# Two transformer layers on one core: the MLP's second products by seven block products, behind all its first products

## The chip, the cores and the metric

The kernel runs on one core of a Trainium2 chip. The metric is device time in microseconds, the median of three runs; before the change it is 3550.99 us (3549.95 to 3551.67). The core has a matmul engine (PE, with its weight loads PEld), three engines for elementwise work (DVE, ACT, POOL), a queue that issues transfers (SP), an on-chip memory (SBUF) and eight accumulation banks (PSUM) into which PE writes.

## What is computed

`x` has 2048 rows of 640. Attention (32 heads of 20) and an MLP follow each other twice, with the same weights in both layers:

```
x = x + attention(layernorm(x), wqkv, wo)
x = x + mlp(layernorm(x), w1, b1, w2, b2)
x = x + attention(layernorm(x), wqkv, wo)
x = x + mlp(layernorm(x), w1, b1, w2, b2)

mlp(y): h = relu(y @ w1 + b1) ** 2        # 2048 x 1536
        out = h @ w2 + b2                 # 2048 x 640
```

All arrays are float32. This document is about the MLP: "first products" are `y @ w1`, "second products" are `h @ w2`.

## The kernel before

**Numbers in two parts.** PE multiplies in a shortened float format. Each operand is therefore split into a high part and the remainder (`split_to`, line 254: ACT casts, DVE subtracts), and every product is made of three matmuls, high x high, high x low and low x high (`THREE`, line 323).

**Memory.** One pool holds 42 slots of 128 partitions x 1024 words ("slot", line 67), a second one 11 tiles of 640 words ("xtile", line 78). The weights lie in pieces, several to a slot, in the class `Split` (line 118). They are split once, on POOL, by `prep_job` (line 838) during the attention of layer one (steps t = 0 to 15 of 32, three times in each), saved to DRAM by `save_full`, and loaded again into slots when a stage needs them. The second weights `w_2` (line 202) are 48 pieces of 320 columns, in 16 slots. The pieces of the first weights `w_1` are 128 columns wide, 120 of them in 15 slots.

**Order.** The program's order is the order on each engine: nothing is rescheduled, and each engine and SP's queue work strictly in turn. Work that is to lie beside matmuls is put between them by hand: a list `steps` of small functions, of which `side()` (line 1364) takes one after each chain of matmuls.

**The MLP.** The rows are taken in four blocks of 512 (`qb`). `mlp` (line 1286) handles one block, in two halves of F (`fh`), six tiles of 128 each. For a tile of F it makes a chain of 15 matmuls of 512 columns into a bank (`chain`, line 333; 5 row groups of `w1` x 3). ACT adds the bias and applies ReLU (line 1301), DVE squares (line 1302), and `split_to` makes the two parts of `h`. After six tiles the second products follow: for each half of the 640 columns (`hf`) and each of four row tiles (`i`) a chain of 18 matmuls of 320 columns, with 128 rows of `h` as the loaded weights and a piece of `w_2` streaming. DVE adds the bank to the row tile `x` (line 1332), to which POOL has added `b2` (line 1308). After the last half SP stores `x`. So first and second products alternate every six tiles, and `h` stays in SBUF.

While a block runs, the next block's rows are loaded, normalised and turned (`turned_rows`, line 302: statistics, scaling and a 32 x 32 transposition on DVE, a trip through DRAM) and split (`parts`, line 292). In the last block of layer one the side work is instead `second()` (line 1403), the front of layer two: normalisation and transposition on PE of its first row blocks (`front`, line 448), with the banks from the ring `ps_all`.

**Counts.** Per block 12 x 15 = 180 first matmuls and 2 x 2 x 4 x 18 = 288 second ones; four blocks and two layers make 1440 and 2304. All of them have line 336 in the profile, told apart by their operands (`xnT,w` and `w,h`).

Of the kernel before, what the change touches and what calls it, by code (L numbers as in the profile page):

```python
# [8 lines left out]
F32 = mybir.dt.float32  # L9
# [7 lines left out]
P = 128  # L17
S = 2048
D = 640
# [2 lines left out]
DH = 20  # L22
KD = D // P
NF = F // P
QB = 512
NQB = S // QB
NG = H // 4
# [6 lines left out]
NBLK = NG * NQB  # L34
NSLOT = 42
NX = 11


@with_exitstack
def tile_layers(  # L40
# [26 lines left out]
    def slot(shape, dtype, label):  # L67
        return arena.tile(shape, dtype, tag="slot", name=name(label))
# [9 lines left out]
    def xtile(label):  # L78
        return xpool.tile([P, D], F32, tag="x", name=name(label))
# [124 lines left out]
    def at_2(f, hw, hf):  # L204

        return (((f // 6) * 2 + hf) * 6 + f % 6) * 2 + hw
# [12 lines left out]

    def put_rows(sp, raw, k, eng_hi, eng_lo):  # L220
        if sp is w_2:
            for hf in range(2):
                part = raw[:, hf * HALF : (hf + 1) * HALF]
                sp.put(part, at_2(k, 0, hf), at_2(k, 1, hf), 1, eng_hi, eng_lo)
        else:
            sp.put(raw, k * 4, k * 4 + 2, 2, eng_hi, eng_lo)

    d_qk = dram.tile([2, 2, D, S], F32R, name="d_qk")
    d_kd = dram.tile([2, 2, 2 * P, QB], F32R, name="d_kd")
# [4 lines left out]
    d_s = dram.tile([NBLK, 4, QB], F32, name="d_s")  # L234
    d_r = dram.tile([NBLK, 4, QB], F32, name="d_r")
    d_t = dram.tile([4, P, D], F32, name="d_t")
    d_x = [dram.tile([S, D], F32, name=f"d_x{i}") for i in range(3)]

    def stats(x):
# [14 lines left out]
    def split_to(dst_hi, dst_lo, src):  # L254

        nc.scalar.copy(dst_hi, src)
        nc.vector.tensor_sub(dst_lo, src, dst_hi.bitcast(F32))
# [62 lines left out]
    def new_rows():  # L320
        return [slot([P, 2, QB], F32R, "xnT") for _ in range(KD)]
# [456 lines left out]
    def finish(t, acc):  # L778
# [52 lines left out]

    jobs = (
        [("o", k) for k in range(KD)]
        + [("1", j) for j in range(NF)]
        + [("2", f) for f in range(NF)]
    )

    def prep_job():

        if raws:  # L840
            kind, i, raw = raws.pop()
            if kind == "1":
                w_1.put(raw, i * 10, i * 10 + KD, KD, pool_hi, pool_lo)
            else:
                put_rows(w_o if kind == "o" else w_2, raw, i, pool_hi, pool_lo)
        if jobs:
            kind, i = jobs.pop(0)
            raws.append((kind, i, raw_cols(w1, i) if kind == "1" else raw_rows(wo if kind == "o" else w2, i)))

# [250 lines left out]
    def attention(first, x_src, first_rows):  # L1100
# [27 lines left out]
        def begin(i):  # L1128

            t, u = divmod(i, NKT)  # L1130
            g, qb = divmod(t, NQB)
            if u == 3:
                q_t.pop(t - 1, None)
            if u == 1:
                if t + 2 < NBLK and t + 2 not in q_t:
                    load_q(t + 2)
            if u % 4 == 1 and qb == 0:
                k_t.pop((g - 1, u // 4), None)
                for h in (0, 1, 2, 3) if g else (1, 2):
# [8 lines left out]
            if first and t < 16 and u == 8:  # L1148
# [134 lines left out]
            xnt.append(t)  # L1283
        return xnt

    def mlp(qb, xnt, x_mid, x_dst, side, nxt):

        xs, res = [], None
        for fh in range(2):
            hs = []  # L1290
            for f in range(fh * 6, fh * 6 + 6):
                dst = ps_all("pu")
                chain(dst, [
                    (w_1.piece(f * 10 + hw * KD + k), xnt[k][:, hx, :])
                    for k in range(KD)
                    for hw, hx in THREE
                ])
                if qb == NQB - 1:
                    w_1.past(f * 10 + 9)
                r = xtile("r")[:, :QB]  # L1300
                nc.scalar.activation(r, dst, AF.Relu, bias=b1_t[:, f : f + 1])  # L1301
                nc.vector.tensor_mul(r, r, r)
                h = slot([P, 2, QB], F32R, "h")
                split_to(h[:, 0, :], h[:, 1, :], r)
                hs.append(h)
                if fh == 0 and f in (1, 2, 3, 4):
                    x = row_tile(x_mid, qb * 4 + f - 1)
                    nc.gpsimd.tensor_add(x, x, b2_t)
                    xs.append(x)
                side()  # L1310
            for hf in range(2):
                c = slice(hf * HALF, (hf + 1) * HALF)
                dsts = [ps_all("y") for _ in range(2)]

                def down(i, part=None):
                    chain(dsts[i][:, :HALF], [
                        (hs[f % 6][:, hx, i * P : (i + 1) * P], w_2.piece(at_2(f, hw, hf)))
                        for f in range(fh * 6, fh * 6 + 6)
                        for hx, hw in THREE
                    ], part)  # L1320

                for i in range(4):
                    if i > 1:
                        dsts.append(ps_all("y"))
                    if hf or i > 1:
                        down(i)
                    elif i == 0:
                        for part in (slice(15), slice(15, 18)):
                            for j in range(2):
                                down(j, part)  # L1330
                    x, dst = xs[i], dsts[i]
                    nc.vector.tensor_add(x[:, c], dst[:, :HALF], x[:, c])
                    if fh == 1 and hf == 1:
                        r0 = (qb * 4 + i) * P
                        dma(nc.sync, x_dst[r0 : r0 + P, :], x)
                    side()
                    if (fh, hf, i) == (1, 0, 0) and nxt:
                        res = new_rows()
                        for j in range(4):
                            parts(res, j, nxt.pop(0))  # L1340
            if fh == 0 and qb == NQB - 1:
                w_2.past(at_2(5, 1, 1))
        return res

    def layer(first, x_a, x_m, x_e, front_0, ahead):
        xs = []
# [34 lines left out]
                all_steps()  # L1381
        w_o.drop()
        xnt = transposed(rows)
        for s in range(w_2.n):
            w_2.load(s)
        for qb in range(NQB):
            rows = []
            if qb + 1 < NQB:
                norm = turned_rows(qb + 1, x_m, rows)
                step = lambda norm=norm: next(norm, None)  # L1390
                both = lambda step=step: (step(), step())
                steps.extend([None] * 6 + [step, both, both, step, step, step, step, both])
            elif ahead:
                some = lambda: [next(ahead, None) for _ in range(2)]
                steps.extend([None] * 7 + [some] * 19 + [lambda: next(ahead, None)])
            xnt = mlp(qb, xnt, x_m, x_e, side, rows if qb + 1 < NQB else None)
            if qb + 1 < NQB:
                all_steps()
        steps.clear()
        w_1.drop()  # L1400
        w_2.drop()

    def second():


        yield from front(0, d_x[1], ps_all)
        for n, _ in enumerate(front(1, d_x[1], ps_all)):
            if n < 5:
                w_qk.load(n)
            yield  # L1410
        yield from front(2, d_x[1], ps_all)
        yield from front(3, d_x[1], ps_q)

    def begin_first():
# [54 lines left out]
```

## Time and profile before

| what | us |
|---|---|
| median of three runs | 3550.99 |
| span of the profiled execution | 3549.7 |
| layer one: projections and attention | to 1373 |
| layer one: output projection | 1373 to 1445 |
| layer one: MLP | 1447 to 1786 |
| layer two: projections and attention | 1786 to 3139 |
| layer two: output projection | 3139 to 3211 |
| layer two: MLP | 3211 to 3546 |

The times of the stages are read from the chain of waits. The profile lists an execution's span; its groups give for each line the engine, the operation, output<-input with shapes, the count, then busy time in us and the mean of one in ns, and the idle time before them with what ended it. A matmul's recorded duration overlaps the next one's, so the spacing of matmuls is read from a run of them, not from the mean.

### The profile page before, as it was taken

How to read it: one execution, taken by the hardware profiler on the slowest of the kernel's cores; microseconds unless marked ns; L12 is line 12 of the kernel's file. 1: busy time of each engine (PE TensorE's matmuls, PEld its weight loads, DVE VectorE, ACT ScalarE, POOL GpSimd, SP SyncE). 2: the span in 40 equal slices, each digit the busy share in tenths (PEclk: the TensorE clock that was granted, in tenths of full speed). 3: DMA queues.
4: the chain of work that ended last, by engine and by line, in shares of the span. 5: the costliest groups of instructions: out<-in, count | busy, mean ns of one | idle time of the engine just before them, and what ended most of it. 6: DMA issues, size and time to landing. Idle time of an engine off the chain costs nothing.

```text
span 3549.7 us, 70872 instructions
## 1 busy us (share of the span) xinstructions
PE 3537.8 (100%) x25544; PEld 2147.2 (60%) x25544; DVE 2631.9 (74%) x5090; ACT 2694.4 (76%) x4712; POOL 820.3 (23%) x935
## 2 busy tenths in 40 slices
PE   9999999999999999999999999999999999999999
PEld 8998333333333336999989973333333333379998
DVE  8999888888888881445579988888888888715443
ACT  5888999999999994122248899999999999932221
POOL 4430344321211210122153201212121211202110
PEclk9999999999999999999999999999999999999999
DMA  7766455423112136622366652222222121366221
GB/s 258 231 209 184 147 167 161 129 76 79 55 48 62 53 103 217 240 75 75 104 205 227 197 165 71 75 79 58 70 82 57 43 60 52 107 233 220 75 82 38
DMA packets 281598, 431.87 MB, mean 122 GB/s; under 512 B 70948, under 2 KB 130084, under 8 KB 281248
## 3 DMA queue, kind: packets, MB, share of 16 engines
q1 hardware_dynamic: 280720, 425.64, 38.6%
q8 instruction: 203, 3.33, 0.4%
q10 hardware_dynamic: 528, 1.70, 0.2%
q14 instruction: 147, 1.20, 0.1%
HBM read 282.52 MB, written 144.68 MB: 120 GB/s over the span
## 4 chain that ended last, share of the span: by engine, by line
PE 96%; DMA 1%; ACT 1%; POOL 1%; issue 0%; SPq 0%; DVE 0%; ACTq 0%; POOLq 0%
PE banks L770 28%; PE banks L336 23%; PE banks L755 18%; PE banks L661 17%; PE banks L368 5%; PE banks L356 5%; PE banks L351 1%; ACT e L765 1%; PE banks L468 0%; SPq L76 0%; DMA d_qk<-ev 0%; DMA x<-in_A_x_dram 0%; DMA q<-d_qk 0%; DMA kd<-d_kd 0%; POOL xnT L271 0%
## 5 line engine op out<-in xcount | busy, mean ns | idle before, releaser
L765 ACT ACTIVATE e<-banks 128x512 f32<-128x512 f32 (+1 forms) x3416 | 2035.0, 691 | 55.6 <-PE banks L755 20.5
L672 DVE TENSOR_REDUCE mx<-banks 128x1 f32<-128x512 f32 x2560 | 1619.7, 684 | 321.0 <-PE banks L661 269.6
L770 PE MATMUL banks<-e,vg 128*32 128x512 f32 x8192 | 1093.4, 605 | 2.3 <-ACT e L765 2.1
L661 PE MATMUL banks<-k,q 60*128 60x512 f32 x3360 | 1059.6, 410 | 0.0
L755 PE MATMUL banks<-q,k 62*128 62x512 f32 x4096 | 1048.9, 441 | 1.3 <-ACT v L432 0.6
L755 PEld LDWEIGHTS banks<-q,k 62*128 62x128 f32 x4096 | 514.7, 184 | 748.3 <-ACT e L765 441.1
L661 PEld LDWEIGHTS banks<-k,q 60*128 60x128 f32 x3360 | 567.9, 185 | 195.4 <-ACT e L765 63.9
L701 DVE CUSTOM_DVE_ANT_0 rl<-banks,rl 128x512 f32<-128x512 f32 x736 | 476.9, 688 | 31.1 <-PE banks L661 6.8
L694 ACT ACTIVATE rl<-banks 128x512 f32<-128x512 f32 x736 | 399.6, 602 | 57.0 <-PE banks L661 45.3
L770 PEld LDWEIGHTS banks<-e,vg 128*32 128x32 f32 x8192 | 162.1, 108 | 353.0 <-issue 271.6
L1301 ACT ACTIVATE r<-banks,b_t 128x512 f32<-128x512 f32 x96 | 66.2, 689 | 364.4 <-PE banks L336 245.8
L336 PE MATMUL banks<-w,h 128*128 128x320 f32 x2304 | 341.2, 309 | 0.0
L336 PEld LDWEIGHTS banks<-w,h 128*128 128x128 f32 x2304 | 339.1, 188 | 1.2
L336 PE MATMUL banks<-xnT,w 128*128 128x512 f32 x1440 | 329.7, 389 | 0.0
L368 PE MATMUL banks<-xnT,wqk 64*128 64x512 f32 x1080 | 326.5, 392 | 0.0
L356 PE MATMUL banks<-xnT,wqk 64*128 64x512 f32 x1080 | 325.6, 393 | 0.0
L336 PEld LDWEIGHTS banks<-xnT,w 128*128 128x128 f32 x1440 | 269.5, 188 | 55.3
L814 POOL TENSOR_TENSOR few<-few,minus_t 128x16 f32<-128x16 f32 x62 | 179.8, 2900 | 234.3 <-DMA few<-d_s 228.5
L661 PE MATMUL banks<-kd,q 60*128 60x512 f32 x736 | 210.8, 398 | 0.8 <-ACT rl L694 0.5
L356 PEld LDWEIGHTS banks<-xnT,wqk 64*128 64x128 f32 x1080 | 199.2, 186 | 13.0 <-issue 1.7
L368 PEld LDWEIGHTS banks<-xnT,wqk 64*128 64x128 f32 x1080 | 201.2, 187 | 7.1
L268 POOL CAST mr<-nt 128x32 fp32r<-128x32 f32 x64 | 13.4, 210 | 813.6 <-DVE nt L727 813.6
(94 smaller groups left out, 2710.2 us busy)
## 6 DMA issues: line engine op xcount, KB each, us to landing
q<-d_qk SPq DMA_DIRECT2D x876, 80.0 KB
d_qk<-ev SPq DMA_DIRECT2D x80, 512.0 KB
k<-d_qk SPq DMA_DIRECT2D x444, 80.0 KB
x<-d_x SPq DMA_DIRECT2D x96, 320.0 KB
d_o<-ot SPq DMA_DIRECT2D x248, 80.0 KB
ot<-d_o SPq DMA_DIRECT2D x38, 512.0 KB
d_v<-v SPq DMA_DIRECT2D x32, 512.0 KB
vg<-d_v SPq DMA_DIRECT2D x32, 512.0 KB
```

What stands on the lines that cost most here:

```text
L336: nc.tensor.matmul(dst, a, b, start=(n == 0), stop=(n == last))
L356: top = nc.tensor.matmul(dst, a[:64], b[:64], start=start, stop=last)
L368: low = nc.tensor.matmul(dst, a, b, start=False, stop=last, skip_group_check=True)
L661: nc.tensor.matmul(dst, q_t[t][b : b + 60, p, sub * P : (sub + 1) * P], k_t[t // NQB, c][b : b + 60, p, :], start=True, stop=True,)
L672: nc.vector.tensor_reduce(maxima(t)[:, 2 * p + par, sub, c : c + 1], dst, axis=AX.X, op=ALU.max)
L694: nc.scalar.activation(r, dst, AF.Relu)
L701: nc.vector.tensor_tensor_reduce(out=r[par], in0=dst, in1=r[par], scale=1.0, scalar=LEAST, op0=ALU.add, op1=ALU.max, accum_out=maxima(t)[: ...
L755: nc.tensor.matmul(dst, k_t[t // NQB, kt // 4][b : b + 62, p, (kt % 4) * P : (kt % 4 + 1) * P], q_t[t][b : b + 62, p, :], start=True, stop ...
L765: nc.scalar.activation(dst, src, AF.Exp, scale=SCALE)
L770: nc.tensor.matmul(acc[32 * h : 32 * h + 32, :], v_t[t // NQB, kt // 8][:, kt % 8, 32 * h : 32 * h + 32], es[p][:, par, :], start=(kt == 0 ...
L814: nc.gpsimd.tensor_tensor(few, few, minus_t, op=ALU.pow)
L1301: nc.scalar.activation(r, dst, AF.Relu, bias=b1_t[:, f : f + 1])
```

## The change

The MLP is rewritten in three respects.

**All first products of a layer come ahead of its second products.** `up` makes the first products of a block. The squared tiles `r` are not split but stored to DRAM (`d_h`), two F tiles to a slot: tile j and tile j + 6, each with 4 row tiles, ordered so that a slot holds for two "units" of 256 rows the four blocks (row tile 0 or 1) x (F half 0 or 1). One sum and one difference that the scheme needs (`s`, and `r[:, :, 2]` in place) are made by DVE there; `s` goes to `d_h1`. A tile's store stands in SP's queue behind the next tile's activation. The stores come after the last addition that writes the tile.

**The second products go by seven block products (Strassen's scheme, in Winograd's form).** The class `Down` takes units of 256 rows: two row tiles, two halves of F, two halves of the columns. Instead of eight block products (144 matmuls) it makes seven (126 matmuls): `W11, T2, T1, T4` into four banks, then, after these have been read out to `u` and to the row tiles, `W21, W22, T3` accumulated onto three of the same banks. Six steps make a unit: two groups x three pairs of F tiles. `make` builds the operands of a step (sums of blocks on DVE, split by ACT and DVE) two steps ahead, `fetch` reads the tiles of the next unit back. Units alternate between banks 0 to 3 and 4 to 7. The addition of `b2` moves from POOL to DVE. In layer one the last 512 rows (two units) are done plainly, 144 matmuls each, in banks 0 to 3, while the front of layer two runs beside them in banks 4 to 7 (`ps_up`); their pieces `W12` are loaded in the place of `T1` to `T4`. In layer two all eight units go by seven products.

**The second weights are kept as eight block sets** instead of four: `W11, W12, W21, W22` and the sums `T1` to `T4`, 96 pieces in 32 slots. `put_pair` makes them from two raw tiles on POOL, in five portions per pair; the preparation therefore runs to step t = 21 (`LAST_PREP`) instead of 15. Pieces of the first weights are put in the order in which `up` uses them (`at_1`).

The diff, cut to its core:

```diff
+NP = NF // 2
+LAST_PREP = 22
...
+    ps_up = Ring(4, 5, 6, 7)
...
-    w_2 = Split("w2", HALF, NF * 4)
+    w_2 = Split("w2", HALF, NP * 16)
...
+    W11, T2, T1, T4, W21, W22, T3, W12 = range(8)
+    SECTIONS = ((W11,), (T2, T1, T4), (W21, W22), (T3,), (W12,))
...
+    def put_pair(f, a, b):
+        t = xtile("t")
+        one, two = slice(0, HALF), slice(HALF, D)
+        def put(p, part):
+            w_2.put(part, at_2(p, f, 0), at_2(p, f, 1), 1, pool_hi, pool_lo)
+        pool_lo(t[:, one], a[:, two], a[:, one])
+        pool_lo(t[:, two], b[:, two], t[:, one])
+        put(W11, a[:, one])
+        yield
+        put(T1, t[:, one])
+        put(T2, t[:, two])
+        yield
...
-            if first and t < 16 and u % 6 == 3:
+            if first and t < LAST_PREP and u % 6 == 3:
                 prep_job()
...
+    def up(qb, xnt, whole, side):
+        held = []
+        def store():
+            while held:
+                r, s = held.pop(0)
+                j = held.pop(0)
+                dma(nc.sync, d_h[qb, j]..., r...)
+                if whole:
+                    dma(nc.sync, d_h1[qb, j]..., s)
+        for j in range(NP):
+            r = slot([P, 2, 4, P], F32, "r")
+            for i in range(2):
+                f = j + i * NP
+                dst = ps_all("pu")
+                chain(dst, [...])
...
+                nc.scalar.activation(r[:, :, i::2, :], ..., AF.Relu, bias=b1_t[:, f : f + 1])
+                if i:
+                    s = None
+                    nc.vector.tensor_mul(r, r, r)
+                    if whole:
+                        s = xtile("s")[:, : 2 * P]
+                        nc.vector.tensor_add(s..., r[:, :, 2, :], r[:, :, 3, :])
+                        nc.vector.tensor_sub(r[:, :, 2, :], r[:, :, 0, :], r[:, :, 2, :])
+                    held.extend([(r, s), j])
+                else:
+                    store()
                 side()
+        return store
...
+        def make(self):
...
+            if grp == 0:
+                s = self.s[un, j]
+                nc.vector.tensor_sub(s[:, 1], s[:, 0], raw[:, :, 0, :])
+                b = self.parts(raw[:, :, 0::3, :], "hb")
+                a = self.parts(s, "ha")
...
+            elif grp == 1:
+                s = self.s.pop((un, j))
+                nc.vector.tensor_sub(s[:, 1], raw[:, :, 1, :], s[:, 1])
+                c = self.parts(raw[:, :, 1:3, :], "hc")
+                d = self.parts(s[:, 1], "hd")
...
+        def run(self, side):
+            for n, (un, grp, j) in enumerate(self.steps):
+                if j == 0 and grp != 1:
+                    b0 = 4 * (un % 2) if grp == 0 else 0
+                    dsts = [banks[:, b0 + b, :HALF] for b in range(4)]
+                    x1, x2 = self.x.pop(un)
+                    for x in (x1, x2):
+                        nc.vector.tensor_add(x, x, b2_t)
...
+                if n + self.LEAD < len(self.steps):
+                    self.make()
+                if grp == 2 or (grp, j) in ((0, 1), (0, 2), (1, 0)):
+                    self.fetch()
...
+                for p, b in order:
+                    for i in range(2):
+                        for hx, hw in THREE:
+                            self.mm(dsts[b], ops[p][:, hx, i],
+                                w_2.piece(at_2(p, lo_f + i, hw)), ...)
+                    if j == last_j:
+                        self.take(un, grp, b, dsts[b], u, x1, x2, c1, c2)
...
+        def take(self, un, grp, b, dst, u, x1, x2, c1, c2):
+            add = nc.vector.tensor_add
+            if grp == 0:
+                if b == 0:
+                    nc.scalar.copy(u[:, 0], dst)
+                elif b == 1:
+                    add(u[:, 1], dst, u[:, 0])
+                elif b == 2:
+                    add(x2[:, c2], dst, x2[:, c2])
+                else:
+                    add(x2[:, c1], dst, x2[:, c1])
+                    add(x1[:, c2], x1[:, c2], u[:, 1])
+            elif b == 0:
+                add(x1[:, c1], dst, x1[:, c1])
+                self.halves(un, x1)
+            elif b == 1:
+                add(u[:, 2], dst, u[:, 0])
+                for c in (c1, c2):
+                    add(x2[:, c], x2[:, c], u[:, 2])
+                self.store(un, 1, x2)
+            else:
+                add(x1[:, c2], dst, x1[:, c2])
+                self.halves(un, x1)
...
+        blocks = NQB if ahead is None else NQB - 1
+        down = Down(blocks, x_m, x_e)
+        coming = [s for s in range(w_2.n) if s not in slots_of(W12)]
...
+                wants = [4, 4, 3, 0, 0, 0, 3, 0, 0, 0, 0, 0] if qb == 0 else [0] * 12
+            else:
+                steps.extend([None] * 5 + [down.fetch, None, down.fetch, lambda: down.rows(0), down.make, down.fetch, down.make])
+                wants = [0, 2, 0, 2, 0, 2, 1, 2, 1, 2, 1, 2]
...
+        down.run(side)
```

More of the change, by code (lines that the diff above doesn't have):

```diff
@@ L220, in put_rows @@
     def put_rows(sp, raw, k, eng_hi, eng_lo):
[L221 to L226, printed above, removed]
+        sp.put(raw, k * 4, k * 4 + 2, 2, eng_hi, eng_lo)
+    def put_pair(f, a, b):
[10 more added lines that the diff above has]
+        yield
+        put(W12, a[:, two])
+        put(W21, b[:, one])
+        yield
+        put(W22, b[:, two])
+        pool_lo(a[:, two], b[:, two], a[:, two])
+        yield
+        put(T3, a[:, two])
+        pool_lo(t[:, two], b[:, one], t[:, two])
+        put(T4, t[:, two])
+        yield
     d_qk = dram.tile([2, 2, D, S], F32R, name="d_qk")
@@ L1298, in mlp @@
                 if qb == NQB - 1:
[L1299 to L1309, printed above, removed]
@@ L1310, in mlp @@
-                side()
[L1311 to L1335, printed above, removed]
-                    side()
[L1337 to L1340, printed above, removed]
@@ new lines, in layer @@
+            all_steps()
+        bring(99)
+        w_1.drop()
+        if ahead:
+            some = lambda: [next(ahead, None) for _ in range(2)]
+            per = 7 * NP // 2
+            one = lambda: next(ahead, None)
+            steps.extend([None] * (per * (2 * blocks - 1)))
+            last = [None] * per
+            for i in (0, 5, 7, 9, 11, 14, 16, 18, 20):
+                last[i] = one
+            last[13] = last[19] = one
+            steps.extend(last + [None] + [one] * 6 + [some] * 11)
@@ L1410, in second @@
             yield
-        yield from front(2, d_x[1], ps_all)
+        yield from front(2, d_x[1], ps_up)
         yield from front(3, d_x[1], ps_q)
```

214 lines of the change are left out of this document (183 added, 31 removed).

## The prediction, made before the changed kernel had run

> **What bounds the kernel now.** I read the page first, then the windows of the two MLP stages, then the chain of waits, then the groups by form. The page:
>
> ```profile
> span 3549.7 us, 70872 instructions
> ...
> PE 3537.8 (100%) x25544; PEld 2147.2 (60%) x25544; DVE 2631.9 (74%) x5090; ACT 2694.4 (76%) x4712; POOL 820.3 (23%) x935
> ...
> PE   9999999999999999999999999999999999999999
> ...
> DVE  8999888888888881445579988888888888715443
> ACT  5888999999999994122248899999999999932221
> ...
> PEclk9999999999999999999999999999999999999999
> ```
>
> PE is busy for 3537.8 of 3549.7 us and its granted clock is full from end to end. DVE and ACT have a quarter free, but that is an average. So I look at the two stages that the change rewrites (columns: stretch, length, busy time and count of PE, PEld, DVE, ACT, POOL, then clock, DMA share, GB/s):
>
> ```profile
> 1447.00:1735.00 288.00, 288.00 (x1622) 263.28 (x1621) 143.54 (x242) 67.50 (x146) 57.77 (x84) 1.00 0.34 115
> ...
> 3211.00:3546.00 335.00, 334.40 (x1889) 305.87 (x1889) 151.88 (x253) 77.36 (x161) 55.27 (x76) 1.00 0.28 97
> ```
>
> Here PE is busy throughout (288.00 of 288, 334.40 of 335) while DVE is at half and ACT at a quarter. The chain of waits (start, length, what) says the same:
>
> ```profile
> 1446.87 288.17 PE banks L336 x1620
> ...
> 1736.35 2.64 PE banks L336 x18
> ...
> 3213.52 332.34 PE banks L336 x1872
> ```
>
> Almost the whole of both MLP stages is one unbroken run of line 336 matmuls, so a matmul taken away is time taken away, so long as no other engine becomes late.
>
> The pace comes from the same rows. A chain of 18 second-product matmuls of 320 columns takes 2.64 us: **146.7 ns each**. The run of 332.34 us in layer two holds 1872 matmuls; 1152 second products at 146.7 ns are 169.0 us, which leaves 163.3 us for 720 first products of 512 columns: 226.8 ns each. The groups give the counts, for both layers together:
>
> ```profile
> L336 PE MATMUL banks<-w,h 128*128 128x320 f32 x2304 | 341.2, 309 | 0.0
> L336 PEld LDWEIGHTS banks<-w,h 128*128 128x128 f32 x2304 | 339.1, 188 | 1.2
> L336 PE MATMUL banks<-xnT,w 128*128 128x512 f32 x1440 | 329.7, 389 | 0.0
> ```
>
> Their means (309 and 389 ns) are longer than the spacing because matmuls overlap; I cost by the spacing.
>
> **What goes.** A unit is 256 rows of output. Plain, it takes 4 output blocks x 12 tiles of F x 3 matmuls = 144 matmuls, 21.12 us. By seven products it takes 7 x 6 x 3 = 126, or 18.48 us. Layer one does 6 units so and 2 plain, layer two does 8 so: 14 x 18 = **252 matmuls fewer, 252 x 0.1467 = 37.0 us**. First products, transposes and attention keep their PE instructions. This is the one gain; everything else below is a question of whether it stays hidden.
>
> The Trainium skill, "TensorE: Matmul & The Clock Gate", section "Back-to-back issue gap", gives an isolated spacing of N/2.4 + 2.5 ns, 135.8 ns at 320 columns, by which an estimate of the saving is 34.2 us; the same section has about 131 ns as a sustained spacing at 512 columns. The trace agrees with neither (146.7 ns at 320 columns, 226.8 at 512), and its spacing stands in the sum.
>
> **What is added: vector and scalar work.** The durations:
>
> ```profile
> L1302 DVE TENSOR_TENSOR r<-r 128x512 f32<-128x512 f32 x96 | 79.5, 828 | 131.2 <-ACT r L1301 129.8 <-DMA y<-d_t 1.3
> L257 DVE TENSOR_TENSOR h<-r,h 128x512 fp32r<-128x512 f32 x96 | 73.7, 767 | 66.0 <-ACT h L256 66.0
> L1301 ACT ACTIVATE r<-banks,b_t 128x512 f32<-128x512 f32 x96 | 66.2, 689 | 364.4 <-PE banks L336 245.8 <-issue 113.6 <-DMA y<-d_t 2.7
> L1332 DVE TENSOR_TENSOR x<-banks,x 128x320 f32<-128x320 f32 x128 | 61.3, 485 | 147.7 <-PE banks L336 132.9 <-POOL x L1308 13.6 <-issue 0.3
> ...
> L256 ACT CAST h<-r 128x512 fp32r<-128x512 f32 x96 | 59.6, 621 | 91.5 <-DVE r L1302 91.5
> L1308 POOL TENSOR_TENSOR x<-x,b_t 128x640 f32<-128x640 f32 x32 | 58.8, 1866 | 165.6 <-DMA x<-d_x 165.6
> ...
> L166 DVE TENSOR_TENSOR wqk<-raw,wqk 128x512 fp32r<-128x512 f32 x1 | 0.7, 685 | 0.0
> ...
> L166 DVE TENSOR_TENSOR wqk<-raw,wqk 128x256 fp32r<-128x256 f32 x1 | 0.4, 418 | 0.0
> ```
>
> ```profile
> L257 DVE TENSOR_TENSOR h<-r,h x96: 691/693/1296, 1452.5 to 3526.9; 128x512 fp32r<-128x512 f32 x96
> ```
>
> With nothing beside it the 128x512 subtraction takes 691 to 693 ns; 256 columns take 418, so one column is 1.04 ns. From that 1024 columns are estimated at 1.22 us and the 640-column bias addition at 0.82 us. Bounds: 0.685 us (512 columns) below, and 1.87 us above, the POOL row that did the same addition; I take 0.82, as it is DVE's own slope.
>
> In a unit by seven products, for each of three pairs of F tiles, the first four products need one 256 subtraction and two 512 ones (1.80 us of DVE), the last three need two of 256 and one of 512 (1.53 us): 3 x 3.33 = 10.0 us. Six additions from PSUM at 0.485 are 2.9 us, three of 320 columns in SBUF at about the same are 1.5 us, and two bias additions, which move here from POOL, are 1.6 us. **DVE: 16.0 us in a unit of 18.48 us**, 87%. ACT copies 3 x (512 + 512 + 512 + 256 columns) at 621 ns per 512, and one bank: some 7 us.
>
> 16.0 fits in 18.48, but DVE works in order, so I follow one unit from PE's start (0). The previous unit's last additions end at 1.5, the bias additions at 3.2, then operands two steps ahead: (first group, pair 2) ready at 5.0, needed at 7.04; (second group, pair 0) 6.5, needed 10.56; pair 1 8.0, needed 13.20. At 8.8 DVE stands behind PE for the evacuations until 11.5; then pair 2 13.1, needed 15.84; the next unit's pair 0 14.9, needed 18.48; pair 1 16.7, needed 22.0. The smallest margin is 2.0 us, so I cost it at nothing. Cover gone (each operation 15% longer), DVE sets the pace. The lead of two steps hides the casts too; the four banks of a unit alternate with the other four, so an evacuation has a whole unit before its bank comes again. Within a unit the second group adds onto three of these banks: bank 0 was copied 2.6 us earlier, bank 2's addition starts two products before and takes 0.49.
>
> In the first products ACT loses the cast (0.62 per tile). DVE loses the subtraction and gains, per pair of tiles, 256 columns twice: 6 x (1.22 + 0.84) = 12.4 us in a block of 180 x 0.2268 = 40.8 us. The next block's rows are normalised there as well:
>
> ```profile
> L244 DVE BATCH_NORM_STATS2 bst<-x 128x6 f32<-128x320 f32 x128 | 54.8, 470 | 21.9 <-DMA x<-d_x 19.2 <-DMA x<-in_A_x_dram 2.7
> ...
> L252 DVE TENSOR_SCALAR x<-x,mv 128x640 f32<-128x640 f32 x40 | 25.3, 659 | 1.3 <-POOL mv L248 1.2
> ...
> L277 DVE TENSOR_SCALAR y<-x,mv 128x640 f32<-128x640 f32 x24 | 22.3, 927 | 0.0
> ...
> L282 DVE STREAM_TRANSPOSE x<-y 128x640 f32<-128x640 f32 x24 | 20.3, 845 | 0.8
> L300 DVE TENSOR_TENSOR xnT<-y,xnT 128x128 fp32r<-128x128 f32 x48 | 20.1, 486 | 0.0
> ...
> L245 DVE BATCH_NORM_AGGREGATE mv<-bst 128x2 f32<-128x12 f32 x64 | 13.4, 209 | 2.2
> ```
>
> Four rows of that: statistics 4 x 1.15, turning 4 x 1.77, splitting 8 x 0.49, 15.6 us. Together 28 of 40.8, and PE has a ring of eight banks. The last row's split is issued a whole chain (3.4 us) before it is needed and takes some 1.5 us of ACT. Cost nothing; if late, 1 to 2 us at three block edges per layer.
>
> **What is added: transfers.** Per layer 24 stores of 512 KB, each read back later as much, and the 128 KB sums with them; 16 more weight slots are saved and 12 to 16 more loaded per layer. In the first-product block that is 3.75 MB per 40.8 us, some 100 GB/s; in a unit 1.9 MB of reads and 1.25 MB of rows, some 180 GB/s. The heaviest stretch now:
>
> ```profile
> 1447.00:1487.00 40.00, 40.00 (x226) 36.48 (x225) 20.24 (x39) 8.60 (x14) 8.99 (x12) 1.00 0.82 318
> ```
>
> 318 GB/s ran beside a PE that did not wait. The last block of layer two, with half of the second weights, tiles and stores, comes to about 13 MB in 40.8 us, near that figure; its last loads are needed only 10 us later. SP's order: a tile's store is queued behind the next tile's activation, and the reads of the next unit wait on the subtractions that free a slot. Behind such a read stand the next row reads and the output stores, which nobody needs within a unit; behind ACT's copy of a bank, which waits for PE, stand casts that are wanted two steps later. The tightest read is issued at 6.5 us of the unit and wanted at 13.1: it is free if it lands in 6.6 us. The nearest row that shows a slow landing is in the chain of waits, a wait for a store:
>
> ```profile
> 1843.80 9.19 DMA d_qk<-ev
> ```
>
> At that, a read would be 2.6 us late per unit, 2.6 x 14 = 36 us. The bytes alone, 640 KB at 318 GB/s, are 2.1 us. The ends are 2.1 and 9.19; I take the margin as enough, since a unit asks for little over half of 318 GB/s, and keep the 36 us for a rival.
>
> Slots: 42. In the first products 15 weight slots + 10 + 14 loaded + 3 for tiles is 42 exactly; in a unit 28 + 3 + 6 to 8 + 1, 38 to 40. Nothing spare, but each slot used again was released at least a step before.
>
> **Attention of layer one** gains POOL work to t = 22: six pairs x (8 splits + 4 subtractions) instead of 24 splits.
>
> ```profile
> L271 POOL TENSOR_TENSOR w<-raw,w 128x320 fp32r<-128x320 f32 x24 | 20.9, 870 | 1.9
> ...
> L268 POOL CAST w<-raw 128x320 fp32r<-128x320 f32 x24 | 10.8, 452 | 19.5 <-DMA raw<-in_B_w_dram 17.2 <-DMA q<-d_qk 2.3
> ```
>
> 84 us instead of 32, so 52 us more. During the present preparation, and after it:
>
> ```profile
> 500.00:600.00 100.00, 100.00 (x717) 38.64 (x717) 83.90 (x140) 97.23 (x166) 42.09 (x53) 1.00 0.50 153
> ...
> 900.00:1000.00 100.00, 100.00 (x718) 38.41 (x716) 83.82 (x138) 97.54 (x166) 19.53 (x18) 1.00 0.21 56
> ```
>
> 717 and 718 PE instructions per 100 us, with POOL at 42 and at 20 us: preparation costs nothing here, and I cost the rest of it at nothing (0 to 1 us).
>
> **Small costs.** At the hand-over from first to second products, the last tile's chain is 0.69 (ACT) + 1.22 + 0.84 + 1.80 = 4.6 us, against 3.52 us of PE work: 0 to 1.0 us per layer, as the first matmuls need only a part; 0.5 each, 1.0 in all. In layer one's last Strassen unit DVE also has the statistics and scaling of four rows (4.6 + 2.6), 22 us in 18.5; the lead of 5.3 us takes most: 0 to 3.5, I take 0.7. The four slots of the second weights that change there must land in 9.7 us: 4 x 480 KB are 6.2 us at 318 GB/s, nothing (3 us, once, if they queue). At the end, now
>
> ```profile
> 3545.89 0.49 DVE L1332 TENSOR_TENSOR x<-banks,x 128x320 f32<-128x320 f32 x1 [2.15 <-PE banks L336]
> ```
>
> the last addition follows the last matmul by one instruction; afterwards three additions stand before it and it ends about 0.2 us later. Sum: 1.9 us.
>
> The profiled execution shows no time but its span. 3549.7 - 37.0 + 1.9 = 3514.6; the median of the runs, 3550.99, is 1.3 above the span, which I add, so **3516 us**, 1.0% faster.
>
> **Rivals.**
> 1. *Late reads or slots*: PE waits a little in every unit. For it: slots full, SP in order. Against: 318 GB/s beside an unhindered PE. At 1 us a unit 3530; at 2.6 us 3552.
> 2. *Conversion sets the pace, and the kernel is slower.* The place is DVE's operand making in the 14 units. It begins when an operation takes 1.15 times its row; the gain is gone when a unit takes 21.12 us, at 16.0 x 1.32. For it, the same operations beside POOL:
>
> ```profile
> L1302 DVE TENSOR_TENSOR r<-r x96: 636/693/2098, 1451.1 to 3525.6; 128x512 f32<-128x512 f32 x96
> ```
>
> and the 1296 ns maximum of line 257. At 1296/693 a unit takes 29.9 us, 14 x 11.4 = 160 more: 3676. Against it: POOL has almost nothing to do in these units, its bias additions being gone. The Trainium skill, "SBUF — State Buffer", section "Who interferes with whom", says that a DVE instruction with two SBUF inputs and a GpSimd instruction that reads SBUF exclude each other for a whole instruction; the trace agrees (2098 against 693 ns), but by that rule an idle POOL costs nothing.
> 3. *The pace of the matmuls rises*, because a bank gets 6 matmuls in a row and not 18, and the load shows. At the load's own 188 ns, 2052 x 41 ns = 84 more: 3600. Against: the bank changes every 18 now and shows no gap.
> 4. *It does not do what it says*: the matmuls go, but waits at block edges and between units give the 37 us back: 3551.
>
> **Chances.** Forecast (3511 to 3524) 0.67; late reads 0.15, at 3530, up to 3545; conversion 0.10, at 3676, of which 0.02 near break-even; pace 0.04; nothing gained 0.04. About 0.2% (7 us) is what a measurement here can tell from no change. Faster 0.82, same 0.06, slower 0.12. The range 3511 to 3545 leaves out 0.18.
>
> **What would show it.** PE unbroken through both stages, 2052 second products at 146.7 ns: right. In the second products, PE waiting for a DVE subtraction (rival 2), with DVE over 95%; for a DMA into a tile, with DVE idle behind it (rival 1); PE busy with spacing over 150 ns (rival 3); attention longer than now, that preparation or slots cost after all. I would be wrong most easily by having summed queues that work in order as if their margins held in every unit.

## The result, and the profile after

The changed kernel takes 3516.18 us (median; 3515.69 to 3517.9) beside 3551.33 us for the kernel before: a ratio of 0.9902, 95% interval 0.9888 to 0.9916. The profiled execution has a span of 3516.1 us. The page of the changed kernel, in its lines for span, busy time and slices:

```profile
span 3516.1 us, 71077 instructions
...
PE 3504.1 (100%) x25292; PEld 2112.9 (60%) x25292; DVE 2732.5 (78%) x5326; ACT 2733.7 (78%) x4804; POOL 828.0 (24%) x975
...
PE   9999999999999999999999999999999999999999
...
DVE  8999888888888882566869988888888888825667
...
PEclk9999999999999999999999999999999999999999
```

PE is still busy almost without a break; DVE has gone from 74 to 78% and ACT from 76 to 78%, and the slices of the MLP, in which DVE had mostly 4 to 5 tenths, now have mostly 5 to 8. The windows of the changed kernel (first and second products of layer one, then of layer two; columns as before):

```profile
1446.00:1610.00 164.00, 164.00 (x729) 135.88 (x727) 90.72 (x151) 47.16 (x114) 32.74 (x60) 1.00 0.76 266
1610.00:1770.00 160.00, 160.00 (x1107) 159.88 (x1106) 123.58 (x248) 55.89 (x103) 16.69 (x29) 1.00 0.59 206
3201.00:3364.00 163.00, 163.00 (x721) 134.99 (x720) 94.21 (x160) 45.99 (x111) 32.36 (x60) 1.00 0.76 266
3364.00:3513.00 149.00, 148.26 (x1009) 147.64 (x1007) 115.55 (x232) 52.55 (x103) 0.00 (x0) 1.00 0.51 173
```

First and second products are now separate stretches, and PE is busy in all of them. The price of keeping `h` in DRAM, and of the added weight slots, is seen in the last column: 266 and 206 GB/s in layer one, 266 and 173 in layer two, where the stretches of the MLP before had 115 and 97. The chain of waits (start, length, what) has line 376 for first and line 1455 for second products:

```profile
1446.62 163.25 PE banks L376 x720
1609.87 114.40 PE banks L1455 x780
...
1769.54 3.44 PE banks L391 x15
...
3125.57 2.39 PE banks L376 x15
...
3200.85 163.23 PE banks L376 x720
3364.08 146.44 PE banks L1455 x996
```

720 first products take 163.25 us, 226.7 ns each, where 226.8 was worked out for the kernel before. The MLP of layer one lasts from 1446.62 to 1769.54, 322.92 us against 338.90. That of layer two begins at 3200.85, and its last matmuls stand in the timeline of PE at the end:

```profile
3511.22 1.04 PE L1455 MATMUL banks<-w,hc 128*128 128x320 f32 x6
```

They end at 3512.26, so the stage lasts 311.41 us against 332.34. Together **36.9 us less**; 252 matmuls at 146.7 ns are 37.0. The groups by form show the count:

```profile
L1455 PE MATMUL banks<-w,hb 128*128 128x320 f32 x504 | 83.2, 309 | 0.0
L1455 PE MATMUL banks<-w,hc 128*128 128x320 f32 x504 | 83.0, 309 | 0.0
L1455 PE MATMUL banks<-w,ha 128*128 128x320 f32 x504 | 80.8, 309 | 0.0
...
L1455 PE MATMUL banks<-w,hd 128*128 128x320 f32 x252 | 43.8, 309 | 0.0
...
L1455 PE MATMUL banks<-w,hh 128*128 128x320 f32 x192 | 42.7, 311 | 0.0
...
L1455 PE MATMUL banks<-w,hl 128*128 128x320 f32 x96 | 29.7, 309 | 0.0
```

504 + 504 + 504 + 252 + 192 + 96 = 2052, where there were 2304.

The span is 33.6 us shorter, not 36.9. The missing 3 us are outside the rewritten stages: layer two's projections and attention took 1353.01 us before (1785.77 to 3138.78) and 1356.03 now (1769.54 to 3125.57). At their start PE stood. The timeline and the window there:

```profile
1788.37 0.79 PE L701 MATMUL banks<-k,q 60*128 60x512 f32 x1 [0.86 <-DMA q<-d_qk]
```

```profile
1786.00:1796.00 10.00, 9.14 (x57) 6.94 (x56) 6.45 (x11) 1.13 (x2) 0.00 (x0) 0.83 0.64 213
```

PE stood 0.86 us for a tile of queries, and the granted clock of those 10 us is 0.83, which is 1.7 us at full clock. Whether the change causes this is one of the questions below.

### The profile page after: what moved, and what is told of

It is laid out like the page before. It is cut to its first block, busy times and chain, and to the rows that moved or that the text cites. A ratio compares the mean times of both kernels' runs of the same rounds, so it can differ in the third digit from the quotient of the medians.

```text
span 3516.1 us, 71077 instructions
## 1 busy us (share of the span) xinstructions
PE 3504.1 (100%) x25292; PEld 2112.9 (60%) x25292; DVE 2732.5 (78%) x5326; ACT 2733.7 (78%) x4804; POOL 828.0 (24%) x975
## 4 chain that ended last, share of the span: by engine, by line
PE 96%; DMA 2%; ACT 1%; POOL 0%; DVE 0%; issue 0%; SPq 0%; POOLq 0%; ACTq 0%; DVEq 0%
PE banks L810 28%; PE banks L795 18%; PE banks L701 18%; PE banks L376 13%; PE banks L1455 9%; PE banks L396 6%; PE banks L408 5%; PE banks L391 0%; PE banks L508 0%; ACT e L805 0%; DMA x<-d_x 0%; DMA x<-in_A_x_dram 0%; SPq L78 0%; DMA few<-d_s 0%; DMA o<-d_r 0%
## 5 line engine op out<-in xcount | busy, mean ns | idle before, releaser
L865 POOL TENSOR_TENSOR o<-o 128x512 f32<-128x512 f32 x62 | 79.6, 1284 | 508.6 <-DMA o<-d_r 285.5
L396 PE MATMUL banks<-wv,xnT 64*128 64x320 f32 x960 | 193.5, 308 | 0.0
```

The source lines that it names most:

```text
L396: top = nc.tensor.matmul(dst, a[:64], b[:64], start=start, stop=last)
```

## The experiments

All start from the changed kernel, and their times stand beside runs of the kernel before on the same chip. The times:

| run | us, median | ratio to before, 95% interval |
|---|---|---|
| e1 all plain | 3551.14 | 0.9999 [0.999, 1.0009] |
| e2 half of layer two's units plain | 3525.47 | 0.9927 [0.9911, 0.9944] |
| e3 operands one step ahead | 3522.95 | 0.9921 [0.9906, 0.9935] |
| e4 three subtractions more | 3517.37 | 0.9904 [0.9888, 0.9921] |
| e5 nine subtractions more | 3546.9 | 0.9988 [0.9979, 0.9997] |
| e6 POOL kept busy | 3619.09 | 1.019 [1.0175, 1.0205] |
| e7 reads doubled | 3596.14 | 1.0126 [1.0111, 1.0141] |
| e9 b2 on POOL | 3519.54 | 0.9909 [0.9894, 0.9924] |
| e10 the same kernel again | 3515.18 | 0.9898 [0.9881, 0.9914] |
| e11 later reads | 3518.38 | 0.9906 [0.9891, 0.992] |

**Is it the matmuls, or the new order?** e1 keeps the order of the changed kernel, with `h` stored and read back, and does every unit plainly. The sums `s` go with the seven products, and only the 16 weight slots of the plain sets are loaded.

```diff
-        blocks = NQB if ahead is None else NQB - 1
+        blocks = 0
-        coming = [s for s in range(w_2.n) if s not in slots_of(W12)]
+        coming = slots_of(W11, W21, W22, W12)
```

The side work of layer two's front keeps its place by units.

> All units are done plainly (2304 second products again), but all first products still come ahead, with h stored to DRAM and read back. Theory (the gain is the 252 matmuls alone, the new order is free): second products back at 1152 x 146.7 ns per layer, time 3516 + 37 = 3553 us, that is 3550 to 3556, like the kernel before. Rival (the new order itself brings or costs something, and the products less or more than 37 us): well away from that, below 3545 if the order brings time, above 3560 if the reads of h cost.

Measured 3551.14 us, the time of the kernel before. In its chain of waits

```profile
1446.44 163.25 PE banks L376 x720
...
1785.19 13.63 PE banks L391 x60
...
3212.97 163.25 PE banks L376 x720
3376.22 168.97 PE banks L1455 x1152
```

1152 second products take 168.97 us, 146.7 ns each, and layer one's MLP lasts 338.75 us (1446.44 to 1785.19) against 338.90. So the order with the stores and reads of `h` is free and brings nothing, to within the 3 us that the interval allows; the gain comes with the products. e2 takes a part of it back:

```diff
-        blocks = NQB if ahead is None else NQB - 1
+        blocks = 2 if ahead is None else NQB - 1
```

> In layer two only four of the eight units go by seven products, the other four plainly; layer one as it is. 4 x 18 = 72 matmuls more than the changed kernel. Theory (each unit by seven products is worth 18 x 146.7 ns = 2.64 us): 3516 + 10.6 = 3527 us, 3525 to 3529. Rival (a fixed part of the gain comes with the scheme, or the last units pay more than the others): below 3521 or above 3533.

Measured 3525.47 us, 9.3 above the first and 10.3 above the second measurement of the changed kernel, where 10.6 were worked out. Its chain:

```profile
3361.71 158.58 PE banks L1455 x1080
```

1080 second products in 158.58 us, 146.8 ns each. The gain goes by units; a fixed part does not show.

**How near is DVE to setting the pace?** The prediction had 16.0 us of DVE in a unit of 18.48. e5 and e4 add to it, by computing low parts twice:

```diff
     def parts(self, src, label):
         t = slot([P, 2] + list(src.shape[1:]), F32R, label)
         split_to(t[:, 0], t[:, 1], src)
+        if label != "hd":            # e4: if label == "hb"
+            nc.vector.tensor_sub(t[:, 1], src, t[:, 0].bitcast(F32))
         return t
```

> The low parts of hb, ha and hc are computed twice, with the same result: 9 more subtractions of 128x512 per unit, 9 x 0.69 = 6.2 us more DVE. Theory (DVE has some 16 us of work in a unit of 18.5, and beyond that it sets the pace): 21.8 to 22.3 us of DVE work per unit, 3.3 to 3.8 us over in each of 14 units, 46 to 53 us: 3562 to 3570 us, DVE nearly always busy in the second products and PE waiting for it. Rival (DVE was far from its limit): under 3530.

> Only the low parts of hb are computed twice: 3 more subtractions per unit, of some 0.62 us each as they follow one another. In the run with nine of them DVE was full and a unit took 20.1 us, which puts the unchanged unit at 14.5 us of DVE. Theory (nothing happens before DVE has 18.5 us): 16.4 us of DVE, no change, 3514 to 3518 us. Rival (the order within the unit leaves less than the sum says): each further us of DVE costs already, 3522 us or more.

e5 took 3546.9 us: the mechanism as the theory has it, but 31 us and not 46 to 53. e4 took 3517.37, 1 to 2 us more than the changed kernel and inside the theory's range. The windows inside layer two's second products, for the changed kernel, e4 and e5 (third column of busy times: DVE):

```profile
3380.00:3500.00 120.00, 120.00 (x820) 120.00 (x819) 94.44 (x190) 42.65 (x84) 0.00 (x0) 1.00 0.51 170
```

```profile
3380.00:3500.00 120.00, 120.00 (x820) 120.00 (x820) 105.52 (x210) 42.52 (x85) 0.00 (x0) 1.00 0.51 170
```

```profile
3400.00:3520.00 120.00, 113.76 (x751) 109.96 (x751) 117.92 (x228) 38.75 (x78) 0.00 (x0) 1.00 0.50 165
```

DVE is busy 94.4, 105.5 and 117.9 of 120 us. A unit of the changed kernel therefore has 0.787 x 18.48 = 14.5 us of DVE, not 16.0. e4 adds 1.7 us to that in each unit. In layer two PE's loads wait for `hb` twice there, 1.1 us in all, in the second and third step of the first unit, and in no later one. Why the durations summed to more is seen in the changed kernel's timeline of DVE:

```profile
3424.46 0.42 DVE L1442 TENSOR_TENSOR s<-r,s 128x256 f32<-128x256 f32 x1
3424.80 0.68 DVE L297 TENSOR_TENSOR hc<-r,hc 128x512 fp32r<-128x512 f32 x1
3425.41 0.42 DVE L297 TENSOR_TENSOR hd<-s,hd 128x256 fp32r<-128x256 f32 x1
```

The subtraction of 0.42 us is followed 0.34 us later by the next one: an instruction's record overlaps the next by some 0.08 us, so a sum of durations is too long by that, some 20 times in a unit. In e5 the waits of PE (engine and line, who it waited for, us in total, times, longest) are

```profile
PE banks L1457 <- ACT u L1541: 4.4, 8, 0.6
PE banks L1457 <- DVE x L1545: 3.9, 8, 0.5
```

PE stands about half a microsecond at a time, where the second group adds onto a bank that DVE or ACT has not yet read; PE's loads, which come ahead of the matmuls, wait 6.5 and 6.0 us at these two places. For operands (`hb` and `ha`), where the prediction pictured the wait, the loads stand only 2.3 us. The operands have two steps of lead, the banks do not.

e3 takes away one of these steps:

```diff
-        LEAD = 2
+        LEAD = 1
-        ..., down.make, down.fetch, down.make])
+        ..., down.make, down.fetch])
```

> Operands are made one step ahead instead of two. By the walk through one unit in the prediction (DVE in order): the operands of step (first group, pair 1) are then made behind the previous unit's last additions and the bias additions, ready at 5.0 us after the unit's start where PE wants them at 3.5; the first product needs only a part of them, so 0.8 to 1.5 us per unit, 14 units: 11 to 21 us, time 3527 to 3537 us, and PE waits for DVE at that step alone. Rival (the margins are wide, two steps are more than is needed): within 3 us of the changed kernel. Rival (the walk is wrong and margins were missing everywhere): over 3550.

Measured 3522.95 us, some 7 us more than the changed kernel, and not 11 to 21. The waits of PE's loads in layer two's second products:

```profile
PEld banks L1455 <- DVE hb L297: 4.2, 8, 1.7
```

PE waits at the place that was named, for `hb` once in each of 8 units, 4.2 us in all with one of 1.7 at the hand-over; the other seven have 0.36 us each. The expectation took the time at which a step's last operand is ready, 5.0 us after the unit's start. In the trace the low part of `hb` is ready after 4.0 us (3426.43, in the unit that begins at 3422.41), and the step's first two matmuls need only the high part.

**What if POOL were busy?** That was the prediction's case for a slower kernel.

```diff
         def make(self):
             n = self.n_op
             self.n_op += 1
             if n >= len(self.steps):
                 return
+            for _ in range(2):
+                nc.gpsimd.tensor_sub(junk, b2_t, b2_t)
```

> With every step of the second products POOL gets two additions of 128x640 whose result nobody uses, 12 in a unit, some 18.6 us of POOL at the 1.55 us of its fastest such row: POOL is nearly always busy beside DVE. Theory (DVE's instructions with two SBUF inputs and POOL's exclude each other, so the prediction's rival 2 fails only because POOL is idle there): DVE loses up to 12 x 1.55 us per unit, 14.5 + 18.6 = 33 us, 14 us over in 14 units: 3640 to 3720 us; at the 1296/693 of the rows 3590 to 3680. Rival (they hardly disturb each other, or only by chance): under 3540 us.

Measured 3619.09 us, 103 us above the changed kernel: far above the rival, below the theory's 3640 to 3720, and inside the 3590 to 3680 that it gives with the slowed rows. The groups of DVE in its second products of layer two, in a stretch where POOL is busy:

```profile
L298 DVE TENSOR_TENSOR hb<-r,hb 128x512 fp32r<-128x512 f32 x9 | 15.6, 1736 | 0.0
L1437 DVE TENSOR_TENSOR s<-s,r 128x256 f32<-128x256 f32 x9 | 13.2, 1469 | 0.0
...
L1544 DVE TENSOR_TENSOR u<-banks,u 128x320 f32<-128x320 f32 x2 | 1.0, 478 | 0.0
```

The 512-column subtraction takes 1736 ns where it took 685 without POOL, and the 256-column one 1469 instead of 419; the addition from a bank, with one operand in SBUF, takes 478, where the changed kernel has 490 to 492. That agrees with the rule of the Trainium skill, "SBUF — State Buffer", section "Who interferes with whom": two SBUF inputs on DVE exclude a POOL instruction that reads SBUF, one does not. One row has two SBUF inputs and keeps 476 ns in both of its cases, `x<-x,u` of line 1549; the first of them starts at 3434.59, just ahead of a POOL instruction that starts at 3434.66. The total fell short of the theory's upper range because POOL did not wait for the units. A window of e6 inside this stretch, and the chain of waits behind it:

```profile
3380.00:3500.00 120.00, 81.90 (x416) 74.06 (x415) 112.83 (x85) 21.70 (x41) 113.94 (x78) 0.86 0.46 162
```

```profile
3508.12 100.75 PE banks L1458 x666
```

While POOL is busy (113.94 of 120 us) PE does 416 matmuls in 120 us, where the changed kernel does 820: a unit takes 36 us, for which the theory had 33. But POOL works through its additions faster than the units come and is done after 3508, and from there on PE does 666 matmuls without a gap. They take 151.3 ns each on average, as the granted clock is 0.50 from 3508 to 3512, 0.71 to 3516, and full after that. e9 is the mild form, the additions of `b2` back on POOL:

```diff
-                        nc.vector.tensor_add(x, x, b2_t)
+                        nc.gpsimd.tensor_add(x, x, b2_t)
```

> The additions of b2 go back to POOL, the rest of the change stays. DVE has 1.6 us less per unit, POOL two instructions of 1.6 to 2.0 us in which DVE's subtractions may stand. Theory (margins of 2 us or more per unit): no change, 3514 to 3519 us. Rival (exclusion by POOL reaches PE): one or two stalls of up to 2 us per unit, 3530 to 3560 us.

Measured 3519.54 us (3517.11 to 3520.6), 4.4 us above e10, which ran on the same chip: far from the rival's 14 and more, but half a microsecond above the theory's range. In layer two the two POOL instructions per unit do not reach PE; the chain of waits has 163.25 and 146.44 us there, where the changed kernel has 163.23 and 146.44. Layer one's MLP is longer, 325.28 us against 323.04 in e10, and the loss lies in its last units. The timeline of DVE, then of SP:

```profile
1723.92 1.74 DVE L1553 TENSOR_TENSOR x<-x,u 128x320 f32<-128x320 f32 x2
```

```profile
1726.14 0.39 SPq L78 DMA_DIRECT2D r<-d_h  x1
```

Beside POOL's addition these two additions take 1.74 us, where the changed kernel has 0.89. The output store waits for them, and the read of a plain unit's tile, behind the store in SP's queue, goes out at 1726.14 instead of 1723.38. Such reads then stand in the chain of waits, and PE waits 1.3 us in four places. So POOL and the late read together do reach PE there. The profile's span is 1.7 us above e10's; where the rest of the 4.4 us lies is not known.

**Do the reads come early enough?** e7 issues each twice into the same slot.

```diff
+            for _ in range(2):
                 dma(nc.sync, raw..., d_h[qb, 2 * j : 2 * j + 2, :, u]...)
```

> Each read of the stored tiles in the second products is issued twice into the same slot, the second behind the first, so that the tile is there 2 us or more later and the reads carry twice the bytes. Theory (a read has 6.6 us before anyone misses it): within 3 us of the changed kernel, 3513 to 3520 us. Rival (reads are near their limit, the prediction's rival 1): each us of lateness costs up to 14 us, over 3530 us, with DVE or ACT waiting for the tile.

Measured 3596.14 us, 80 us above the changed kernel. The expectation was wrong, but so was the experiment: SP's waits in layer two's second products show what it tested.

```profile
SPq L78 <- DMA r<-d_h: 126.2, 24, 8.7
```

The second read of a slot waits for the first to land, on SP, and SP works in order: 24 waits of 5.3 us on average, 126 us in which it issued nothing else. So it says how long a read takes to land there, and not what the bytes cost. e11 asks again, by issuing the reads two steps later.

```diff
-                if grp == 2 or (grp, j) in ((0, 1), (0, 2), (1, 0)):
+                if grp == 2 or (grp, j) in ((1, 0), (1, 1), (1, 2)):
```

> The reads of the next unit's tiles are issued two steps later, in the last three steps of a unit instead of its second to fourth. In the run with doubled reads SP stood 126.2 us in 24 waits for the first of two reads, so one read takes some 5.3 us to land (8.7 at most). Theory (a read has time to spare, and that run was slow because SP stood still for each landing): the first tile is asked for 10.6 us after the unit's start, is there at 15.9, its operands at 17.6, wanted at 18.5: 3514 to 3522 us. Rival (reads are near their limit): at 8.7 us each unit is 2.6 us late, 3551 us, and PE waits behind a DMA.

Measured 3518.38 us, 2 to 3 us more than the changed kernel. Its timeline, of SP and then of DVE, in a unit of layer two:

```profile
3430.65 0.36 SPq L78 DMA_DIRECT2D r<-d_h  x1
3431.06 0.47 SPq L78 DMA_DIRECT2D s<-d_h  x1
```

```profile
3436.35 0.42 DVE L1434 TENSOR_TENSOR s<-s,r 128x256 f32<-128x256 f32 x1 [0.88 <-DMA s<-d_h]
```

`s` was asked for at 3431.06 and DVE had it at 3436.35: 5.3 us to land, and DVE stood 0.88 us, which reached PE nowhere in layer two. In layer one there is one place where a read did, ahead of the plain units. First the chain of waits, then the timeline of PE:

```profile
1710.63 9.98 DMA r<-d_h
```

```profile
1721.78 0.56 PE L1455 MATMUL banks<-w,hh 128*128 128x320 f32 x2 [0.88 <-ACT hh L296]
1723.04 0.41 PE L1455 MATMUL banks<-w,hl 128*128 128x320 f32 x1 [0.70 <-DVE hl L297]
```

The tile took 9.98 us there, and PE stood 0.88 and 0.70 us for its two parts. Two waits of 0.41 us follow, and layer one's MLP takes 326.25 us, 3.2 more than in e10.

The changed kernel's reads are issued much earlier than the prediction had it. In its timeline of SP, in a unit whose first matmul starts at 3419.7,

```profile
3421.80 0.38 SPq L78 DMA_DIRECT2D r<-d_h  x1
...
3422.82 0.48 SPq L78 DMA_DIRECT2D r<-d_h  x1
...
3426.80 0.37 SPq L78 DMA_DIRECT2D r<-d_h  x1
```

they go out 2.1, 3.1 and 7.1 us after the start; the prediction had 6.5 for the first, because it let them wait for the subtraction that frees a slot. In the trace the first two follow directly behind the previous unit's output stores, which SP issues from 3419.53 to 3421.69, and which wait for DVE's additions (line 1553: 25.9 us of SP's waits in 8 times). Only the third waits for a subtraction (`hd`, line 297: 12.0 us, 6 times). That slots were free for the first two is what I take from it; no run shows it by itself.

**Were the 3 us an accident?** e10 is the same kernel with a second profile.

> The changed kernel once more, for a second profile. In the first one layer two's projections and attention took 1356.0 us where before they took 1353.0: PE stood 0.86 us for a transfer and then ran some 3 us at half its clock. Theory (an accident of that one execution): 1353 to 1354 us in this profile, and a span of 3513 to 3515 us with the same median, 3515 to 3518. Rival (the new end of layer one causes it): 1356 us again, span 3516.

Its median is 3515.18 us, its span 3513.6. Chain and window of that profile:

```profile
1769.86 13.63 PE banks L391 x60
...
3123.51 2.40 PE banks L376 x15
```

```profile
1786.00:1796.00 10.00, 10.00 (x77) 7.93 (x78) 6.94 (x12) 3.21 (x6) 2.07 (x2) 1.00 0.62 211
```

1353.65 us from 1769.86 to 3123.51, no wait, clock 1.00. So the long wait is not in every execution: of the changed kernel's eight timed runs only the profiled one of the first four has a granted clock below 1.00 (0.999), and the other seven have spans of 3512.8 to 3514.6. That the change has no part in it is not shown: in e4's profile PE waits 0.28 us for the same tile at the same place, while the kernel before has no such wait in its profile and a granted clock of 1.00 in all 33 runs beside the experiments. The margin there seems to be small now, and why the transfer was later by a microsecond once stays open. Without the wait the span is 36.1 us shorter than before; of the 0.8 us that are missing from 36.9, 0.6 lie in layer two's projections and attention, with no cause found.

## Why the prediction was right, point by point

- **What bounds the kernel**: right. PE was the only engine that mattered in these stages; e1 shows that the work around it, with traffic of 219 and 159 GB/s in layer one's two stretches, costs nothing as long as it stays beside PE.
- **252 matmuls at 146.7 ns, 37.0 us**: right, 36.9 measured in the two stages, and 146.7 to 146.8 ns in e1 and e2. The bank that changes every six matmuls does not alter the pace: 820 matmuls in 120 us (rival 3 falls).
- **DVE hides**: right, but its work was put at 16.0 us per unit and is 14.5, because durations overlap. The margin is wider: e4 adds 1.7 us a unit and in layer two PE waits for it only in the first unit, e5 with 9 x 0.62 = 5.6 sets the pace, 14.5 + 5.6 = 20.1 us a unit (its window has 751 matmuls where there were 820: 20.2). Break-even was put at 21.1 us; e5 is 4.3 us short of the kernel before, 0.3 per unit, so it lies nearer 20.5. This is an estimate, as the ends of the stages pay too: in layer one's last unit by seven products e5 has a wait of 2.53 us, and from 1727 to 1731 the granted clock is 0.50.
- **Reads hide**: right, but for a reason that was not in the sum. The first read goes out 4.4 us earlier than was worked out; such a read lands in 5.3 us (e11), between the ends of 2.1 and 9.19. Rival 1's place is real as well: two steps later, and layer one's last reads reach PE (e11, and to a smaller part e9).
- **Small costs, 1.9 us**: not found. The hand-over costs 0.2 us (below), layer one's last unit by seven products nothing (the stage lost 15.98 us, 108 matmuls are 15.8), and the end nothing: span less last matmul is 3.84 us before and after. The forecast span of 3514.6 us stands against 3516.1 in the first profile, with its wait, and 3513.6 in e10. That the median came out at 3516.18 against 3516 is therefore partly luck: the stalls were too many, and the distance from a run's span to its time, taken as 1.3, is 1.8 (3515.38 against 3513.6 in e10).
- **Preparation and slots in attention**: right at nothing; layer one's MLP begins at 1446.62 against 1446.87. What the prediction did not cost is the start of layer two's attention, where the first profile lost its 3 us.
- **Rival 2, the slower kernel**: its mechanism is real (e6) and its place too; it needs a POOL that works, and the change took POOL's work away there. That little is left over at layer one's end is seen in e9.

The waits of PE's loads in layer two's second products of the changed kernel, the 0.2 us of the hand-over:

```profile
PEld banks L1455 <- DVE hb L297: 0.2, 1, 0.2
```

## What to carry to other kernels

Where one engine has no idle time, count its instructions and price them by their spacing in an unbroken run; the rest of a change is then only a list of covers, each to be checked against the time at which someone misses it. Work that is added to other engines is free up to a point that one can find by adding more of it: two extra doses (e4, e5) place it better than a sum. Two waits that a sum does not show are the ones in order on a queue (SP in e7) and the banks that are written again within the same unit (e5).

## What the runs showed of the hardware

- Records of DVE instructions that follow each other overlap by some 0.08 us: 0.42 us long, 0.34 us apart.
- A subtraction with both inputs in SBUF goes from 685 to 1736 ns beside a POOL that reads SBUF all the time, one of 320 columns with an input in PSUM takes 478 ns there, and 490 to 492 with POOL idle.
- After a wait of 0.86 us in the first profile PE's granted clock was 0.83 over 10 us, which is 1.7 us at full clock, twice the wait itself. Waits of 0.88 and 0.70 us in e11 were followed by none of that: the clock is 1.00 from 1720 to 1735.
- PE kept its spacing of 226.7 ns beside transfers of 266 GB/s for 163 us.
